# Rearranging the first slots of a fused top-k attention and MLP kernel

## The chip, the cores and the metric

The kernel runs on one core of one Trainium2 chip. The metric is device time in microseconds (us) of one execution, and the median of several runs is compared. Five engines with queues of their own take part: TensorE (PE in the profile), VectorE (DVE), ScalarE (ACT), GpSimd (POOL), and SyncE (SP), which here only issues DMAs. Each works strictly in the order of its queue (weight loads of TensorE can be pulled ahead, row "PEld").

## The reference

For 8 batches of 8 heads, 576 tokens and head size 64: scores, the 32 largest scores of each row kept, softmax over those, times V. The heads are then put side by side (512 features for each of 4608 tokens) and an MLP with 2048 hidden features follows, whose negative half is scaled by a vector alpha.

```
scores = (q @ k.T) / sqrt(64)
kth    = 32nd largest of each row
attn   = softmax(where(scores >= kth, scores, -1e9))
x      = attn @ v                     # heads side by side: 4608 x 512
h      = x @ w_in                     # 4608 x 2048
g      = max(h, 0) + alpha * min(h, 0)
out    = g @ w_out                    # 4608 x 512
```

The kernel writes g as (1 - alpha) * max(h, 0) + alpha * h. The first part uses w_out scaled by (1 - alpha), `w_out_b`. The second is linear in x, so a 512 x 512 matrix `w_lin_b` = w_in (alpha * w_out) is computed once at the start, from `w_la` = alpha * w_out and from a transposed copy of w_in.

## The kernel before, in words

**Units of work.** Two heads form a pair; 4 pairs are a batch, 32 pairs in all. A duo is one 128-row block of both heads of a pair, `("n", pair, j)` with j from 0 to 3, or the 64-row tails of two pairs together, `("m", pair, pair)`. There are 18 duos to a batch and 144 in all; the list `duos` sets their order.

**Slots.** The loop `for n in range(ND + 6)` writes one slot after the other, and each slot touches duos at different stages: scores of duo n+2 on TensorE (`st_qk`, tile `ps_sc`, one buffer); their copy to SBUF on ScalarE for n+1 (`st_exit_1`, `st_exit_0`, tile `s_sb`); the search for the 32nd largest on VectorE (`dve_slot`: twelve MAX8 over 96 columns for duo n, two MAX8 over 576 columns, `p<-y`, for duo n-1); the sign pass `sg` on ScalarE and the product `y` on GpSimd for n-1; `r` on ScalarE and the subtraction `s_sb<-s_sb,r` on GpSimd for n-2; exp (tile `w`) on ScalarE and a DMA transpose of it issued by SyncE (`wT<-w`) for n-3; times V on TensorE (`st_av`, tile `xo`) and the norm on VectorE (`rz`, `x`) for n-5. Every engine has the whole slot in its queue in that order, so a late operand holds all that stands behind it. The instruction `TENSOR_SCALAR p<-small` stands once near the end of VectorE's part of each slot, and its start marks the slot's end in the rows below: there are 144 of them, for slots 0 to 143.

**The MLP beside it.** When both halves of a 256-token chunk are transposed (`st_xT`), `mlp_ready` puts 8 hidden units (`unit`, tile `ph`, 8 matmuls, then one VectorE instruction `gT<-ph`) and 8 output parts (`part`, tile `pz`, 5 matmuls) in lists; `h_pe`, `h_dve` and `o_pe` put about one of each into a slot, two where the list is long. The last two 128-row chunks have 4 units each. What is left when the duos end runs behind the last slot. Where a slot has no unit or part, `keep_warm` puts 4 matmuls in its place (tile `idle`), from slot 4 on.

**Preparing a pair.** `load_one` loads k, q or v (3 DMAs; three staging buffers for k and q, two for v). `prep_pe(p, u)` transposes k (u=0), q (u=1) and both tails (u=2) on TensorE into `tps`, `prep_evac` copies that to `qkT` on ScalarE or VectorE, and `cast_v` casts v on GpSimd, which frees the staging buffer of v.

**The weights.** `out_load(i)` (SyncE) brings 1 MB of w_out to `w_st`, `scale_out(f)` makes one 128x512 block each of `w_out_b` (ScalarE) and `w_la` (VectorE), `w_in_load` (GpSimd's queue) brings w_in, `in_trans` (SyncE) transposes it, `lin` makes `w_lin_b` on TensorE. The dictionary `todo` holds these, filled by `at(slot, kind, f)`; `run(n, kind)` writes them at their place in slot n ("ld" first, "cast" and "prep" late, "scale" last). So SyncE's queue in slot n is: loads of the slot, stores, the transpose of exp(n-3), the transposes of x.

Of the kernel before, what the change touches and what calls it, by code (L numbers as in the profile page):

```python
# [35 lines left out]
def fast_path(tc, q, k, v, moe_w_in, moe_w_out, moe_alpha, out, flag):  # L36
# [17 lines left out]
    for b in range(B):  # L54
        p0 = KPB * b
        full = [("n", p, j) for j in range(4) for p in range(p0, p0 + KPB)]
        tails = [("m", p0, p0 + 1), ("m", p0 + 2, p0 + 3)]
        duos += full + tails if b < B - 1 else tails + full
    ND = len(duos)
# [3 lines left out]
    with ExitStack() as ctx:  # L63
# [3 lines left out]
        io = pool("io", 2)  # L67
        qk_p = pool("qk", 2 * KPB)
        s_p = pool("s", 5)
# [29 lines left out]
        load_one(0, "q", ACT)  # L99
        load_one(1, "k", SP)  # L100
        load_one(1, "q", ACT)

# [334 lines left out]
        def keep_warm():  # L437

            ps = ps_h.tile([128, 512], FP32, name="idle", tag="h")
            for i in range(4):  # L440
                PE.matmul(ps, v1s[0][:, 0, :, :].rearrange("p a b -> p (a b)")[:, 0:128], ws[0][:, 0, 0:512],
                          start=(i == 0), stop=(i == 3))
# [35 lines left out]
        def at(slot, kind, f):  # L478
            todo.setdefault((max(0, slot), kind), []).append(f)

        for b in range(1, B):
            for i in range(KPB):
                p = KPB * b + i
                s0 = NB * (b - 1) + 15 * i // 4
                at(s0 - 6, "ld", lambda p=p: load_one(p, "k"))
                at(s0 - 5, "ld", lambda p=p: load_one(p, "q"))
                at(s0 + 2, "ld", lambda p=p: load_one(p, "v"))
                at(s0 + 5, "cast", lambda p=p: cast_v(p))
                for u in range(3):
                    at(s0 + u, "prep", lambda p=p, u=u: prep_pe(p, u))  # L490
        for p in range(KPB):
            at(p + 1 + p // 2, "cast", lambda p=p: cast_v(p))
            if p > 1:
                at(p, "ld", lambda p=p: load_one(p, "v"))

        def w_in_load(i):
            POOL.dma_start(w_in_b[i], moe_w_in[128 * i:128 * i + 128, :])
# [7 lines left out]
        def scale_out(f):  # L505
            if f % 8 == 0:
                hold["wl", f // 8] = gp.tile([128, 8, 512], BF16, name="w_la", tag="gT")
            src = hold["st", f // 4][:, f % 4, :]
            ACT.activation(w_out_b[f // 4][:, f % 4, :], src, AF.Copy, scale=alpha1m[:, f:f + 1])
            DVE.tensor_scalar(hold["wl", f // 8][:, f % 8, :], src, alpha_sb[:, f:f + 1], None, ALU.mult)  # L510

# [21 lines left out]
        for i in range(4):  # L533
            at((0, 1, 5, 9)[i], "ld", lambda i=i: out_load(i))
            at(3 + 2 * i, "w", lambda i=i: w_in_load(i))
        for f in range(NFT):
            at(1 + f, "scale", lambda f=f: scale_out(f))
        for kk in range(4):
            at((13, 14, 17, 18)[kk], "ld", lambda kk=kk: in_trans(kk))
            for a in range(2):  # L540
                at(16 + 2 * kk + a, "lin", lambda kk=kk, a=a: lin(kk, a))
            at(18 + 2 * kk, "lin_out", lambda kk=kk: lin_out(kk))

# [7 lines left out]

        load_one(2, "k")
        load_one(2, "q")
        load_one(0, "v")
        load_one(3, "k")
        load_one(3, "q")
        load_one(1, "v")

        def prep_all(p, *copies):
            prep_pe(p, 0)  # L560
            prep_pe(p, 1)
            prep_evac(copies[0])
            prep_evac(copies[1])
            prep_pe(p, 2)
            prep_evac(copies[2])


        warm = ps_z.tile([128, 128], FP32, name="warm", tag="z")
        for i in range(12):
            PE.transpose(warm, ident_f, ident_f)  # L570
        prep_all(0, DVE.tensor_copy, ACT.copy, DVE.tensor_copy)
        st_qk(0)
        st_exit_1(0)
        st_exit_0(0)
        prep_all(1, DVE.tensor_copy, ACT.copy, ACT.copy)
        st_qk(1)
        aps = ps_z.tile([128, NFT], FP32, name="aps", tag="z")
        PE.transpose(aps, a16, ident_f[0:NFT, 0:NFT])
        ACT.copy(alpha_sb, aps)
        ACT.activation(alpha1m, aps, AF.Copy, scale=-1.0, bias=1.0)  # L580

        for n in range(ND + 6):
# [5 lines left out]
            if on(n - 5):  # L588
                st_av(n - 5)
            if not h_pe() and not end and n > 3:  # L590
                keep_warm()
# [18 lines left out]
            run(n, "lin_out")  # L610
            if n < 2:
                prep_all(2 + n, ACT.copy, ACT.copy, ACT.copy)
            run(n, "prep", 1)
            if on(n + 2):
                st_qk(n + 2)
            if (n, "lin") in todo:
                run(n, "lin")
            elif not did and not end and n > 3:
                keep_warm()
            elif end or (ready() > 9 and oq[0][1] < NFT):  # L620
                o_pe()
            if on(n - 3):
                st_exp(n - 3)
            while pend:
                prep_evac(ACT.copy)
            run(n, "scale")
# [301 lines left out]
```

## Time and profile before

| what | value |
|---|---|
| runs | 899.44 us median of 3 (898.17, 899.44, 903.78) |
| the profiled execution | 901.29 us, span 899.5 us |
| busy over the span | PE 778.6, DVE 793.8, ACT 791.8, POOL 749.2 us |
| mean granted TensorE clock | 0.952 of full speed |
| busy share of VectorE in 40 slices of 22.5 us | 0.3 and 0.6 in the first two, 0.7 to 0.8 in the next five, 0.9 or more up to the 38th |
| granted clock in those slices | 0.6 to 0.8 in the first seven, 0.9 or more behind |

The profile is of one execution; its times are counted from the start of its span. Busy time is what an engine worked; a wait is put down to the event that ended it. [...]

### The profile page before, as it was taken

How to read it: one execution, taken by the hardware profiler on the slowest of the kernel's cores; microseconds unless marked ns; L12 is line 12 of the kernel's file. 1: busy time of each engine (PE TensorE's matmuls, PEld its weight loads, DVE VectorE, ACT ScalarE, POOL GpSimd, SP SyncE). 2: the span in 40 equal slices, each digit the busy share in tenths (PEclk: the TensorE clock that was granted, in tenths of full speed). 3: DMA queues.
4: the chain of work that ended last, by engine and by line, in shares of the span. 5: the costliest groups of instructions: out<-in, count | busy, mean ns of one | idle time of the engine just before them, and what ended most of it. 6: DMA issues, size and time to landing. Idle time of an engine off the chain costs nothing.

```text
span 899.5 us, 18557 instructions
## 1 busy us (share of the span) xinstructions
PE 778.6 (87%) x5350; PEld 461.3 (51%) x5350; DVE 793.8 (88%) x4063; ACT 791.8 (88%) x1448; POOL 749.2 (83%) x662
## 2 busy tenths in 40 slices
PE   7767777988989889988988899988988999998886
PEld 5423333555555555655455555655555544654553
DVE  3666877899999999999999999999999999999931
ACT  2857787989999999999999999999999999999820
POOL 1766788779999899999999999999998999998910
PEclk6667789999999999999999999999999999999999
DMA  7857675545655556665666465675555444444341
GB/s 159 192 88 140 136 148 114 112 87 91 131 112 109 117 113 121 118 112 103 140 123 116 91 129 104 117 119 112 111 121 108 94 91 93 75 86 77 78 91 39
DMA packets 341006, 99.36 MB, mean 110 GB/s; under 512 B 333712, under 2 KB 333728, under 8 KB 340896
## 3 DMA queue, kind: packets, MB, share of 16 engines
q1 hardware_dynamic: 337888, 95.40, 53.4%
q0 software_dynamic: 608, 2.11, 1.5%
q10 hardware_dynamic: 2400, 0.59, 0.4%
q8 instruction: 44, 0.72, 0.3%
q14 instruction: 66, 0.54, 0.2%
HBM read 36.71 MB, written 9.44 MB: 51 GB/s over the span
## 4 chain that ended last, share of the span: by engine, by line
DVE 33%; ACT 25%; PE 22%; POOL 7%; issue 6%; DMA 5%; SPq 1%; ACTq 0%; POOLq 0%
DVE small L31 9%; DVE p L31 9%; ACT sg L31 7%; PE ps_sc L31 6%; ACT r L31 6%; DVE up L31 5%; ACT w L31 5%; ACT s_sb L31 5%; PE pz L31 5%; POOL y L31 4%; DVE gT L31 4%; PE xo L31 4%; PE ph L31 3%; DMA wT<-w 3%; PE idle L31 2%
## 5 line engine op out<-in xcount | busy, mean ns | idle before, releaser
L31 POOL TENSOR_TENSOR y<-s_sb,sg 128x576 f32<-128x576 f32 x288 | 362.0, 1278 | 89.0 <-ACT sg L31 87.6
L31 POOL TENSOR_TENSOR s_sb<-s_sb,r 128x576 f32<-128x576 f32 x288 | 364.8, 1285 | 19.0 <-ACT r L31 18.2
L31 PE MATMUL ps_sc<-qkT 64*128 64x128 f32 (+7 forms) x1280 | 265.4, 461 | 85.5 <-ACT s_sb L31 82.1
L31 PEld LDWEIGHTS ps_sc<-qkT 64*128 64x128 f32 (+1 forms) x1280 | 148.3, 182 | 227.6 <-ACT s_sb L31 138.2
L31 DVE MAX8 p<-y 128x8 f32<-128x576 f32 x288 | 215.9, 750 | 18.8 <-POOL y L31 18.1
L31 ACT ACTIVATE r<-s_sb,KT 128x576 bf16<-128x576 f32 x288 | 228.4, 794 | 3.8 <-DVE KT L31 2.6
L31 ACT ACTIVATE sg<-s_sb,p 128x576 bf16<-128x576 f32 x288 | 223.1, 786 | 6.2 <-DVE p L31 5.7
L31 DVE MAX8 small<-s_sb 128x8 f32<-128x96 f32 x864 | 217.0, 251 | 0.0
L31 ACT COPY s_sb<-ps_sc 128x576 f32<-128x576 f32 x288 | 184.6, 641 | 34.3 <-PE ps_sc L31 33.3
L31 DVE MAX8 up<-s_sb 128x8 f32<-128x96 f32 x864 | 212.4, 246 | 2.3 <-ACT s_sb L31 2.3
L31 ACT ACTIVATE w<-s_sb 128x1152 bf16<-128x1152 f32 x144 | 168.3, 1169 | 10.3 <-POOL s_sb L31 8.6
L31 PE MATMUL ph<-xT,w_in_b 128*128 128x256 bf16 (+1 forms) x1216 | 150.7, 268 | 0.8 <-DVE gT L31 0.8
L31 PE MATMUL pz<-w_out_b,gT 128*128 128x512 bf16 x576 | 149.6, 383 | 0.0
L31 PE MATMUL xo<-v,wT 128*128 128x65 bf16 (+3 forms) x1600 | 128.7, 200 | 18.6 <-DMA wT<-w 17.0
L31 PEld LDWEIGHTS <-wT 128*128 128x128 bf16 (+3 forms) x1600 | 91.5, 100 | 67.1 <-DMA wT<-w 21.4
L31 PEld LDWEIGHTS <-w_in_b 128*128 128x128 bf16 x1216 | 104.1, 98 | 19.7 <-issue 0.8
L31 DVE TENSOR_SCALAR gT<-ph 128x512 bf16<-128x512 f32 x144 | 97.3, 676 | 18.2 <-PE ph L31 18.1
L31 PEld LDWEIGHTS <-gT 128*128 128x128 bf16 x576 | 56.8, 99 | 57.7 <-issue 6.4
L31 ACT ACTIVATION_READ_ACCUMULATOR sg<-s_sb,p 128x1 f32 x288 | 59.7, 207 | 0.0
L31 PE MATMUL pz<-w_lin_b,xT 128*128 128x512 bf16 x144 | 56.3, 391 | 3.8 <-ACT o_sb L31 3.8
L31 ACT COPY qkT<-tps 128x512 f32<-128x512 f32 (+1 forms) x93 | 44.5, 482 | 6.1 <-PE tps L31 6.0
L31 DVE RECIPROCAL rz<-xo 128x2 f32<-128x2 f32 x144 | 22.7, 157 | 29.6 <-PE xo L31 29.0
(49 smaller groups left out, 592.6 us busy)
## 6 DMA issues: line engine op xcount, KB each, us to landing
k_st<-in_k_dram SPq DMA_DIRECT2D x64, 128.0 KB, 2.8
v_st<-in_v_dram SPq DMA_DIRECT2D x64, 128.0 KB, 2.6
out_dram<-o_sb SPq DMA_DIRECT2D x32, 256.0 KB, 2.5
q_st<-in_q_dram SPq DMA_DIRECT2D x60, 128.0 KB, 2.8
w_st<-in_moe_w_out_dram SPq DMA_DIRECT2D x4, 1024.0 KB, 6.8
wT<-w SPq DMA_TRANSPOSE x144, 3.5
w_in_b<-in_moe_w_in_dram POOLq DMA_DIRECT2D x4, 512.0 KB, 6.6
k_st<-in_k_dram SPq DMA_DIRECT2D x32, 32.0 KB, 2.6
```

The source lines that it names most:

```text
L31: return self.tc.keep_in_program_order(f(*a, **kw))
```

## The change

- **Order of the duos.** Before: row block 0 of the four pairs, then block 1, 2, 3, then the tails. Now: blocks 0 and 1 of a pair in turn, pair by pair, then blocks 2 and 3 the same way, then the tails. In the last batch the tails stood first; now they stand behind blocks 0 and 1, and blocks 2 and 3 follow one by one. A new pair is thus first used every second slot instead of every slot.
- **The opening.** Only pair 0 is prepared ahead of the first scores, and scores of duo 1 (the same pair) come ahead of the transposes of pair 1. `prep_all` for pairs 2 and 3 in slots 0 and 1 is gone; their transposes are spread over slots 0 to 3, two steps a slot. q of pair 1 is loaded by SyncE instead of ScalarE. An Exp on a constant is put first in ScalarE's queue.
- **Loads, casts and transposes.** Slots moved; for all later batches a pair is now prepared every 4 slots. `qk` has 7 buffers instead of 8.
- **The weights.** Loads, `scale_out` (two a slot in slots 3 to 6), `in_trans` and `lin` moved.
- **The alpha product.** The instruction that makes `w_la` sees source and result as 256 x 2 elements, the two 256 columns apart, instead of 512 in a row.
- **keep_warm.** Runs in every slot from 0 on; in slots 0 to 5 it makes 4 transposes of the 128x128 identity instead of 4 matmuls. Ten more warm-up transposes stand in the opening.

```diff
-        full = [("n", p, j) for j in range(4) for p in range(p0, p0 + KPB)]
+        last = b == B - 1
+        half = lambda j, n: [("n", p, j + i) for p in range(p0, p0 + KPB) for i in range(n)]
         tails = [("m", p0, p0 + 1), ("m", p0 + 2, p0 + 3)]
-        duos += full + tails if b < B - 1 else tails + full
+        duos += half(0, 2) + tails + half(2, 1) + half(3, 1) if last else half(0, 2) + half(2, 2) + tails
...
-        qk_p = pool("qk", 2 * KPB)
+        qk_p = pool("qk", 2 * KPB - 1)
...
         load_one(0, "k", SP)
         load_one(0, "q", ACT)
-        load_one(1, "k", SP)
-        load_one(1, "q", ACT)
+        for p in range(1, 3):
+            load_one(p, "k", SP)
+            load_one(p, "q", SP)
+        load_one(0, "v", SP)
...
             for i in range(4):
+                if now[0] < 6:
+                    PE.transpose(ps[:, 128 * i:128 * i + 128], ident_f, ident_f)
+                    continue
...
-                s0 = NB * (b - 1) + 15 * i // 4
-                at(s0 - 6, "ld", lambda p=p: load_one(p, "k"))
-                at(s0 - 5, "ld", lambda p=p: load_one(p, "q"))
+                s0 = NB * (b - 1) + 4 + 4 * i
+                at(s0 - 3, "ld", lambda p=p: load_one(p, "k"))
+                at(s0 - 2, "ld", lambda p=p: load_one(p, "q"))
                 at(s0 + 2, "ld", lambda p=p: load_one(p, "v"))
                 at(s0 + 5, "cast", lambda p=p: cast_v(p))
...
         for p in range(KPB):
-            at(p + 1 + p // 2, "cast", lambda p=p: cast_v(p))
-            if p > 1:
-                at(p, "ld", lambda p=p: load_one(p, "v"))
+            at(2 * p + 2, "cast", lambda p=p: cast_v(p))
+            if p:
+                at(2 * p - 1, "ld", lambda p=p: load_one(p, "v"))
+        for u in range(3):
+            at(u // 2, "prep", lambda u=u: prep_pe(2, u))
+            at(2 + u // 2, "prep", lambda u=u: prep_pe(3, u))
...
-            DVE.tensor_scalar(hold["wl", f // 8][:, f % 8, :], src, alpha_sb[:, f:f + 1], None, ALU.mult)
+
+            DVE.tensor_scalar(hold["wl", f // 8][:, f % 8, :].rearrange("p (a b) -> p b a", a=2),
+                              src.rearrange("p (a b) -> p b a", a=2), alpha_sb[:, f:f + 1], None, ALU.mult)
...
-            at((0, 1, 5, 9)[i], "ld", lambda i=i: out_load(i))
+            at((1, 3, 5, 8)[i], "ld", lambda i=i: out_load(i))
...
-            at(1 + f, "scale", lambda f=f: scale_out(f))
+            at(3 + f // 2 if f < 8 else f - 1, "scale", lambda f=f: scale_out(f))
...
+        ACT.activation(alpha1m, ident_f[:, 0:NFT], AF.Exp)
+        heat(14)
+        for u in range(2):
+            prep_pe(0, u)
+        prep_evac(DVE.tensor_copy)
+        prep_pe(0, 2)
+        prep_evac(ACT.copy)
+        prep_evac(DVE.tensor_copy)
+        heat(6)
+        st_qk(0)
+        load_one(3, "k")
+        load_one(3, "q")
         st_exit_1(0)
         st_exit_0(0)
-        prep_all(1, DVE.tensor_copy, ACT.copy, ACT.copy)
+        heat(2)
         st_qk(1)
+        for u in range(2):
+            prep_pe(1, u)
+        prep_evac(DVE.tensor_copy)
...
-            if not h_pe() and not end and n > 3:
+            if not h_pe() and not end:
                 keep_warm()
...
-            if n < 2:
-                prep_all(2 + n, ACT.copy, ACT.copy, ACT.copy)
-            run(n, "prep", 1)
+            run(n, "prep", 2 if n < 4 else 1)
```

Three places of the queues, before and now. First SyncE's queue from the load of v for pair 3 (slot 3) to the transpose of exp of duo 2 (slot 5) (`v_st`, `k_st`, `q_st` are staging tiles; `w_st` is 1 MB of w_out; `wT<-w` the transposes of exp). Before:

```order
L31 DMA v_st<-in_v_dram 128x4x64 x2
L31 DMA v_st<-in_v_dram 64x2x64
L31 DMA_TRANSPOSE wT<-w_141 128x10x128
L31 DMA_TRANSPOSE wT<-w_142 128x10x128
L31 DMA v_st<-in_v_dram 128x4x64 x2
L31 DMA v_st<-in_v_dram 64x2x64
L31 DMA k_st<-in_k_dram 128x4x64 x2
L31 DMA k_st<-in_k_dram 64x2x64
L31 DMA w_st<-in_moe_w_out_dram 128x4x512
L31 DMA_TRANSPOSE wT<-w_143 128x10x128
```

Now, up to the transpose of exp of duo 3:

```order
L31 DMA w_st<-in_moe_w_out_dram 128x4x512
L31 DMA_TRANSPOSE wT<-w_155 128x10x128
L31 DMA v_st<-in_v_dram 128x4x64 x2
L31 DMA v_st<-in_v_dram 64x2x64
L31 DMA q_st<-in_q_dram 128x4x64 x2
L31 DMA q_st<-in_q_dram 64x2x64
L31 DMA_TRANSPOSE wT<-w_153 128x10x128
```

In the first piece the load ahead of the first transpose is v of pair 3 in slot 3, and the one behind the second is v of pair 5 in slot 5. In the second the v load is that of pair 4 in slot 6, which takes the buffer that the cast of pair 2 frees in the same slot.

TensorE's queue from the first scores on, the first piece of the difference (`warm` and `idle` are transposes of the identity, `tps` transposes of k and q, `ps_sc` scores):

```order
 L31 MATMUL tps<-ident_f,q_st 128x64
+L31 MATMUL warm<-ident_f 128x128 x6
 L31 MATMUL ps_sc<-qkT 128x512
 L31 MATMUL ps_sc<-qkT 128x448
 L31 MATMUL ps_sc<-qkT 128x128
 L31 MATMUL ps_sc<-qkT 128x64
+L31 MATMUL warm<-ident_f 128x128 x2
+L31 MATMUL ps_sc<-qkT 128x512
+L31 MATMUL ps_sc<-qkT 128x448
+L31 MATMUL ps_sc<-qkT 128x128
 L31 MATMUL tps<-ident_f,k_st 128x128 x4
 L31 MATMUL tps<-ident_f,q_st 128x128 x4
```

The scores of duo 1 moved ahead of the transposes of pair 1, and eight identity transposes came in.

VectorE's queue at the end of slot 4 (`pk` is the last small step of a slot, `up<-s_sb` the first MAX8 of the next). Before:

```order
L31 TENSOR_SCALAR w_la<-w_st,alpha_sb 128x512
L31 MAX up<-s_sb 128x8
L31 MAX small<-s_sb 128x8
L31 TENSOR_REDUCE KT<-pk 128x2
L31 MAX up<-s_sb 128x8
```

Now:

```order
L31 TENSOR_SCALAR w_la<-w_st,alpha_sb 128x256x2 x2
L31 MAX up<-s_sb 128x8
L31 MAX small<-s_sb 128x8
L31 TENSOR_REDUCE KT<-pk 128x2
L31 MAX up<-s_sb 128x8
```

Two alpha products stand there in slots 3 to 6, one in slots 7 to 14; before there was one in each of slots 1 to 16. Behind the last scores in TensorE's queue stand 7 units of the 256-token chunks and 25 output parts before, 12 and 26 now; with the 8 units of the last two chunks that is 15 and 20 units.

## Rows read from the trace of the kernel before

**Rows 1.** Windows view: columns stretch, length, busy (instructions) per engine, granted clock, DMA, GB/s.

```profile
17.00:51.00 34.00, 23.40 (x85) 14.28 (x86) 24.36 (x101) 25.46 (x51) 20.14 (x20) 0.65 0.66 154
51.00:103.00 52.00, 35.77 (x165) 17.56 (x164) 34.72 (x173) 35.13 (x64) 33.80 (x35) 0.73 0.75 147
103.00:170.00 67.00, 55.92 (x321) 28.53 (x319) 52.70 (x278) 57.25 (x105) 52.76 (x45) 0.89 0.59 118
```

**Rows 2.** Timeline of VectorE: start, us, then the instruction; ends of slots 0, 20, 118, 119.

```profile
16.94 0.16 DVE L31 TENSOR_SCALAR p<-small 128x2 f32<-128x2 f32 x1
...
169.79 0.14 DVE L31 TENSOR_SCALAR p<-small 128x2 f32<-128x2 f32 x1
...
711.95 0.15 DVE L31 TENSOR_SCALAR p<-small 128x2 f32<-128x2 f32 x1
...
716.68 0.15 DVE L31 TENSOR_SCALAR p<-small 128x2 f32<-128x2 f32 x1
```

**Rows 3.** Waits of VectorE from 17 to 170: us in total, times, longest.

```profile
DVE rz L31 <- PE xo L31: 19.0, 11, 4.2
DVE p L31 <- POOL y L31: 11.0, 15, 2.7
...
DVE w_la L31 <- DMA w_st<-in_moe_w_out_dram: 3.5, 1, 3.5
```

**Rows 4.** Timelines of ScalarE, SyncE and TensorE around the first transpose of exp.

```profile
40.38 1.15 ACT L31 ACTIVATE w<-s_sb 128x1152 bf16<-128x1152 f32 x1
...
51.47 1.57 SPq L31 DMA_DIRECT2D v_st<-in_v_dram  x3
53.14 3.63 SPq L31 DMA_TRANSPOSE wT<-w  x2
...
56.87 1.06 PE L31 MATMUL xo<-v,wT 128*128 128x65 bf16 x10 [4.73 <-DMA wT<-w]
```

**Rows 5.** Timelines of VectorE and GpSimd: alpha products and what GpSimd ran beside one.

```profile
41.85 4.92 DVE L31 TENSOR_SCALAR w_la<-w_st,alpha_sb 128x512 bf16<-128x512 f32 x1
...
60.64 0.48 DVE L31 TENSOR_SCALAR w_la<-w_st,alpha_sb 128x512 bf16<-128x512 f32 x1
...
93.76 2.45 DVE L31 TENSOR_SCALAR w_la<-w_st,alpha_sb 128x512 bf16<-128x512 f32 x1
...
227.99 0.68 DVE L31 TENSOR_SCALAR gT<-ph 128x512 bf16<-128x512 f32 x1
...
41.49 2.52 POOL L31 TENSOR_TENSOR s_sb<-s_sb,r 128x576 f32<-128x576 f32 x2
43.97 2.50 POOL L31 TENSOR_TENSOR y<-s_sb,sg 128x576 f32<-128x576 f32 x2
```

**Rows 6.** Timeline of ScalarE: two exps one slot apart, copy between them, a weight product.

```profile
228.71 1.20 ACT L31 ACTIVATE w<-s_sb 128x1152 bf16<-128x1152 f32 x1
229.77 0.61 ACT L31 COPY qkT<-tps 128x512 f32<-128x512 f32 x1
...
234.17 1.20 ACT L31 ACTIVATE w<-s_sb 128x1152 bf16<-128x1152 f32 x1
...
30.93 0.72 ACT L31 ACTIVATE w_out_b<-w_st,alpha1m 128x512 bf16<-128x512 f32 x1 [0.59 <-DMA w_st<-in_moe_w_out_dram]
```

**Rows 7.** Timeline of TensorE in slots 5 and 6, at either clock.

```profile
61.10 2.29 PE L31 MATMUL ps_sc<-qkT 64*128 64x512 f32 x6 [0.52 <-ACT s_sb L31]
63.32 1.89 PE L31 MATMUL idle<-w,v 128*128 128x512 bf16 x4
65.00 1.09 PE L31 MATMUL xo<-v,wT 128*128 128x65 bf16 x10
...
68.28 1.24 PE L31 MATMUL ps_sc<-qkT 64*128 64x512 f32 x6 [0.73 <-ACT s_sb L31]
```

**Rows 8.** Timeline of TensorE at the end: two units with one part between them.

```profile
847.38 1.05 PE L31 MATMUL ph<-xT,w_in_b 128*128 128x256 bf16 x8
...
849.34 0.93 PE L31 MATMUL ph<-xT,w_in_b 128*128 128x256 bf16 x7
```

More of the change, by code (lines that the diff above doesn't have):

```diff
@@ L533, in fast_path @@
         for i in range(4):
-            at((0, 1, 5, 9)[i], "ld", lambda i=i: out_load(i))
-            at(3 + 2 * i, "w", lambda i=i: w_in_load(i))
+            at((1, 3, 5, 8)[i], "ld", lambda i=i: out_load(i))
+            at((3, 6, 8, 10)[i], "w", lambda i=i: w_in_load(i))
         for f in range(NFT):
-            at(1 + f, "scale", lambda f=f: scale_out(f))
+            at(3 + f // 2 if f < 8 else f - 1, "scale", lambda f=f: scale_out(f))
         for kk in range(4):
-            at((13, 14, 17, 18)[kk], "ld", lambda kk=kk: in_trans(kk))
+            at((11, 12, 15, 16)[kk], "ld", lambda kk=kk: in_trans(kk))
             for a in range(2):
-                at(16 + 2 * kk + a, "lin", lambda kk=kk, a=a: lin(kk, a))
-            at(18 + 2 * kk, "lin_out", lambda kk=kk: lin_out(kk))
+                at(15 + 2 * kk + a, "lin", lambda kk=kk, a=a: lin(kk, a))
+            at(17 + 2 * kk, "lin_out", lambda kk=kk: lin_out(kk))
         def run(n, kind, most=99):
@@ L549, in run, with heat @@
                 todo.setdefault((n + 1, kind), [])[0:0] = l[most:]
-        load_one(2, "k")
-        load_one(2, "q")
-        load_one(0, "v")
+        warm = ps_z.tile([128, 128], FP32, name="warm", tag="z")
+        def heat(m):
+            for _ in range(m):
+                PE.transpose(warm, ident_f, ident_f)
+        ACT.activation(alpha1m, ident_f[:, 0:NFT], AF.Exp)
[8 more added lines that the diff above has]
+        st_qk(0)
         load_one(3, "k")
         load_one(3, "q")
[L557 to L572, printed above, removed]
         st_exit_1(0)
         st_exit_0(0)
-        prep_all(1, DVE.tensor_copy, ACT.copy, ACT.copy)
+        heat(2)
         st_qk(1)
+        for u in range(2):
+            prep_pe(1, u)
+        prep_evac(DVE.tensor_copy)
+        prep_evac(ACT.copy)
+        prep_pe(1, 2)
+        prep_evac(ACT.copy)
         aps = ps_z.tile([128, NFT], FP32, name="aps", tag="z")
         PE.transpose(aps, a16, ident_f[0:NFT, 0:NFT])
-        ACT.copy(alpha_sb, aps)
-        ACT.activation(alpha1m, aps, AF.Copy, scale=-1.0, bias=1.0)
         for n in range(ND + 6):
@@ L617, in fast_path @@
                 run(n, "lin")
-            elif not did and not end and n > 3:
+            elif not did and not end:
                 keep_warm()
@@ L624, in fast_path @@
             while pend:
-                prep_evac(ACT.copy)
+                prep_evac(DVE.tensor_copy if n < 4 and len(pend) == 1 else ACT.copy)
+            if n == 1:
+                ACT.copy(alpha_sb, aps)
+                ACT.activation(alpha1m, aps, AF.Copy, scale=-1.0, bias=1.0)
             run(n, "scale")
```

## The prediction

> **What bounds the kernel now.** I read the 40 slices first: VectorE and ScalarE are full from about 160 us to the end of the slots, and thin before. The windows view puts numbers on the thin stretch [rows 1]: from 17 to 170 us VectorE worked 24.36 + 34.72 + 52.70 = 111.8 of 153 us, ScalarE 117.8 by the same sum, and the granted clock was 0.65, 0.73 and 0.89. Then I took the end of each slot from VectorE's timeline [rows 2]. Slot 0 ends at 16.94 and slot 20 at 169.79, so slots 1 to 20 took 152.9 us, 7.64 each. What a slot needs stands in the same view far behind: slot 119, which has no hidden unit, took 716.68 - 711.95 = 4.73 us without a gap on VectorE. So the opening is the place where time can come from, and a change to the opening can give at most the difference between 152.9 us and what the busiest engine needs there.
>
> That need is ScalarE's. From exp to exp it took 5.46 us with one 0.61 us copy of a transposed q or k in it, 4.85 without [rows 6]. Slots 1 to 20 of the changed kernel hold 20 x 4.85 = 97.0, sixteen weight products of 0.72 [rows 6] = 11.5, and 14 copies that stay on ScalarE, at most 0.61 each, 8.5: 117 us. VectorE needs 111.8 less what it lost in two stretched alpha products (below), about 105. So **the ceiling of the gain is 152.9 - 117 = 36 us**.
>
> Next I read what VectorE waited for [rows 3]: 41.2 us idle (153 - 111.8), of which 19.0 for the product with V (`rz<-xo`), 11.0 for `y`, 3.5 for the first weights. Behind the first of these stands SyncE's queue [rows 4]: exp of duo 0 ended at 41.53, but its transpose was issued at 53.14, right behind a v load that had waited for a buffer. TensorE got it at 56.87. The v load held the transpose for 11.6 us.
>
> **The change part by part,** against the profiled execution of 901.29 us.
>
> *Weights later.* The first `w_st` is loaded in slot 0 and used in slot 1, and VectorE waited 3.5 us [rows 3]. Now two slots lie between load and use: -3.5.
>
> *Loads of v and the transposes behind them.* The v load of slot 3 takes a buffer whose cast is now in slot 2, where before three loads fought for two buffers up to slot 5. One load of this kind is left: v of pair 4 in slot 6 waits for the cast of the same slot, with q of pair 5 and the transpose of exp of duo 3 queued behind it, and TensorE's product in slot 8 waits for that. The 1 MB loads of w_out in slots 5 and 8 also still stand ahead of a transpose. I take half of the 19.0 us [rows 3]: -9.5. Bounds: -19.0 if the queue never blocks again; 0 if the loads left cost what the old ones did.
>
> *Copies ahead of the sign pass.* Six copies for pairs 2 and 3 stood in slots 0 and 1, ahead of `sg`; now they are spread over four slots and VectorE takes some. Of the 11.0 us for `y`, -4; of the idle time that remains (41.2 - 19.0 - 11.0 - 3.5 = 7.7, much of it where TensorE prepares two pairs in a row), -4. Bounds together 0 and -18.7.
>
> *The alpha product.* Fourteen of the sixteen took about what the one at 60.64 took, 0.48; two took 4.92 and 2.45 [rows 5]. The long one ran from 41.85 to 46.77, while GpSimd worked without a gap from 41.49 to 46.47: VectorE stood until GpSimd was done. 0.48 us for 512 elements is also short of the 0.68 that 512 elements from PSUM take [rows 5], so it runs in a faster form that seems to need something GpSimd holds. The two cost 4.44 + 1.97 = 6.4 us. If the new view ends that, -6.4; if the product then takes 0.68, it costs 16 x 0.20 = +3.2. Bounds for one product: 0.48, as now, and 4.92, the longest seen. I take 0.68, the nearest row for 512 elements one by one.
>
> [...]
>
> *The first microseconds.* VectorE now copies a part of pair 1 ahead of its slot 0, and the scores of duo 1 (1.24 us at full clock, 2.29 at half [rows 7]) stand ahead of those transposes; against it, ScalarE is ready earlier because it issues three DMAs fewer. I take +1.5, bounds -1.2 and +4.
>
> *More keep_warm.* Eight identity transposes a slot in slots 0 to 3. Eight matmuls of 512 columns took at most 2 x 1.89 [rows 7], which is the upper bound; TensorE had 34.0 - 23.4 = 10.6 us free from 17 to 51 [rows 1], 2.6 a slot. I cost them at nothing while that holds; without it at 1.2 a slot, 5 in all.
>
> *Between slot 21 and the last batch.* The work of a batch is the same and the spacing of loads 4 slots instead of 3.75: 0, bounds -4 and +3.
>
> *The end.* The last batch's tails now become ready behind blocks 0 and 1, so 5 more units and 1 more part run after the last scores. A unit and a part took 849.34 - 847.38 = 1.96 there, a further unit at most 1.05 [rows 8]: 1.96 + 4 x 1.05 = +6.2 where TensorE sets the end. The slots lose 5 VectorE instructions of 0.68 [rows 5], up to -3.4. I take +3.5, bounds +2.8 and +6.2.
>
> Sum: -3.5 - 9.5 - 4 - 4 - 6.4 + 3.2 + 1.5 + 0 + 3.5 = **-19.2**, so 882.1 for an execution like the profiled one. That one lay 1.85 above the median of the runs, 899.44, so the median should be about **880**.
>
> **The rivals.**
>
> 1. *The alpha product still waits for GpSimd* (the change doesn't do what it says). For it: nothing in the trace shows that it was the order of the elements that let it run in 0.48 us; and with shorter slots GpSimd, 106.7 of 153 us busy by the sum of its column [rows 1], would be nearer 85%, and two products now stand together in slots 3 to 6. Against it: the time of a strided stream is not in the trace. Five long products instead of two, at the mean loss of (4.44 + 1.97) / 2 = 3.2 us, cost 16.0, against a gain of 6.4 less 3.2 in my sum: 882.1 + 16.0 - 3.2 = 895 in the profile if nothing hides it, and about 888 where ScalarE hides half; median 887. Chance 0.15. [...]
>
> 2. *The waits move.* ScalarE or TensorE comes late in place of the queue, and the three middle terms (17.5) give half: +8.8, profile 891, median 889. For it: a chain through TensorE, ScalarE and GpSimd runs through each early slot, and a wait removed shows the next. Against it: the ceiling of 36 us is far above what I take. Chance 0.17.
>
> 3. *TensorE at half clock becomes the bound: slower.* The place is slots 6 to 18, where two `idle` groups a slot remain. [...] It decides where the mean granted clock of that stretch falls below about 0.7. For it: the clock was 0.73 from 51 to 103, and the new fillers of slots 0 to 5 are short transposes. Against it: it rose to 0.89 behind [rows 1], as the gaps on TensorE became shorter, and the change makes gaps shorter. Chance 0.08.
>
> **How the numbers follow.** My forecast has 0.60. The low end is the ceiling: 36 us less, the same work at the end, a median near 864. The high end takes in rivals 1 and 2 with their bounds, 897; it leaves out rival 3 and a little at both ends. A difference of under 1%, 9 us, I count as no change: that is, faster means below 890.4. The forecast lies there nearly wholly (0.57 of 0.60), rival 1 with 0.10 of 0.15, rival 2 with 0.08 of 0.17. Faster 0.75, within 1% 0.17, slower 0.08.
>
> **What would show it.** In the changed profile slot 20 should end near 146 to 150 instead of 169.79; the first transpose of exp should be issued within 2 us of its exp; no alpha product should last over 1 us; `rz<-xo` should hold VectorE for about 10 us in the opening, with its longest wait near slot 8; the stretch behind the last slot should be 4 to 6 us longer than now. The prediction is wrong if slot 20 ends after 160, if the alpha products are stretched as before, or if the slots between 21 and 125 change their pace, of which I count on nothing.

## The result, and the profile after

The changed kernel took **876.1 us** (median of 4 runs, 874.74 to 877.41) against 899.63 (4 runs, 898.17 to 903.78): a ratio of **0.9729, interval 0.9699 to 0.976**. The profiled execution took 874.74 us with a span of 873.0 (901.29 and 899.5 before), at a mean granted clock of 0.973 (0.952). The forecast was 880. The time came out near it, but two of its terms were wrong by over ten microseconds each, in opposite directions, and the experiments were spent on that.

The timeline of VectorE in the changed kernel gives the ends of slots 0, 3, 20, 125 and 143, which answer to [rows 2] (start, duration, instruction):

```profile
16.84 0.16 DVE L31 TENSOR_SCALAR p<-small 128x2 f32<-128x2 f32 x1
...
31.93 0.14 DVE L31 TENSOR_SCALAR p<-small 128x2 f32<-128x2 f32 x1
...
151.72 0.14 DVE L31 TENSOR_SCALAR p<-small 128x2 f32<-128x2 f32 x1
...
725.45 0.14 DVE L31 TENSOR_SCALAR p<-small 128x2 f32<-128x2 f32 x1
...
822.30 0.15 DVE L31 TENSOR_SCALAR p<-small 128x2 f32<-128x2 f32 x1
```

In the kernel before, slots 0 and 20 end at 16.94 and 169.79 [rows 2], and slots 3, 125 and 143 here:

```profile
41.63 0.14 DVE L31 TENSOR_SCALAR p<-small 128x2 f32<-128x2 f32 x1
...
750.90 0.14 DVE L31 TENSOR_SCALAR p<-small 128x2 f32<-128x2 f32 x1
...
848.99 0.14 DVE L31 TENSOR_SCALAR p<-small 128x2 f32<-128x2 f32 x1
```

Set beside each other, the two sets of five divide the 26.5 us of the span:

| stretch | before, us | after, us | difference |
|---|---|---|---|
| to the end of slot 0 | 16.94 | 16.84 | -0.1 |
| slots 1 to 3 | 24.69 | 15.09 | -9.6 |
| slots 4 to 20 | 128.16 | 119.79 | -8.4 |
| slots 21 to 125 | 581.11 | 573.73 | -7.4 |
| slots 126 to 143 | 98.09 | 96.85 | -1.2 |
| behind the last slot | 50.51 | 50.70 | +0.2 |

The windows view of the changed kernel, for slots 1 to 20, answers to [rows 1] (stretch, length, busy time of PE, PEld, DVE, ACT and POOL with instructions, granted clock, DMA share, GB/s):

```profile
17.00:51.00 34.00, 22.85 (x120) 15.03 (x117) 33.69 (x136) 26.99 (x52) 25.49 (x23) 0.80 0.66 163
51.00:103.00 52.00, 40.95 (x210) 20.87 (x209) 49.59 (x199) 41.19 (x75) 45.99 (x38) 0.77 0.82 158
103.00:152.00 49.00, 42.41 (x255) 22.29 (x255) 43.96 (x222) 45.77 (x84) 41.81 (x36) 0.93 0.58 115
```

VectorE, the third figure, is now full in the first two stretches: 33.69 of 34 and 49.59 of 52. By the sum it worked 127.2 of 135 us, where it had worked 111.8 of 153. So its idle time fell from 41.2 to 7.8 us, **33.4 less**, while its busy time rose by **15.4**. The gain of these slots, 18.0 us, is the difference of the two. What is left of the idle time stands in VectorE's waits from 17 to 152 (us in total, times, longest), against [rows 3]:

```profile
DVE p L31 <- POOL y L31: 2.9, 7, 1.2
DVE rz L31 <- PE xo L31: 2.6, 4, 1.1
DVE small L31 <- ACT sg L31: 1.6, 3, 0.9
```

The wait for the product with V went from 19.0 to 2.6, that for `y` from 11.0 to 2.9, and that for the first weights is gone. The busy time is the alpha products'. The groups view of VectorE in the same stretches shows their sum and the mean of one, first before, then in the changed kernel:

```profile
L31 DVE TENSOR_SCALAR w_la<-w_st,alpha_sb 128x512 bf16<-128x512 f32 x16 | 14.8, 924 | 3.5 <-DMA w_st<-in_moe_w_out_dram 3.5
```

```profile
L31 DVE TENSOR_SCALAR w_la<-w_st,alpha_sb 128x512 bf16<-128x512 f32 x16 | 34.5, 2267 | 0.0
```

Their rows grew by 19.7 us. That is more than the 15.4 by which the busy time rose, because 3.9 us more of them overlap the rows of neighbouring instructions.

The timelines of VectorE and GpSimd show two kinds of product, and answer to [rows 5]:

```profile
32.34 7.03 DVE L31 TENSOR_SCALAR w_la<-w_st,alpha_sb 128x512 bf16<-128x512 f32 x2
...
58.04 4.13 DVE L31 TENSOR_SCALAR w_la<-w_st,alpha_sb 128x512 bf16<-128x512 f32 x2
...
73.56 1.54 DVE L31 TENSOR_SCALAR w_la<-w_st,alpha_sb 128x512 bf16<-128x512 f32 x1
...
88.19 3.51 DVE L31 TENSOR_SCALAR w_la<-w_st,alpha_sb 128x512 bf16<-128x512 f32 x1
...
34.27 2.50 POOL L31 TENSOR_TENSOR y<-s_sb,sg 128x576 f32<-128x576 f32 x2
40.44 2.55 POOL L31 TENSOR_TENSOR s_sb<-s_sb,r 128x576 f32<-128x576 f32 x2 [3.67 <-ACT r L31]
42.92 0.85 POOL L31 CAST v<-v_st 128x512 bf16<-128x512 f32 x2
...
58.98 3.34 POOL L31 CAST v<-v_st 128x512 bf16<-128x512 f32 x2
```

No product took under 1.5 us; the shortest took 1.54, three times the 0.48 of before. The pair at 32.34 took 7.03 beside a product `y` that kept its usual 2.50: VectorE stood. GpSimd was then idle for 3.67 us, because the `r` that it needed waited for VectorE. Beside the pair at 58.04 it was the other way round: two casts of v took 3.34 us, against 0.85 at 42.92, and GpSimd stood. So the two engines still hold each other up, and the new element order made each product longer.

The queue of SyncE, on the other hand, did what the prediction said. ScalarE's exp of duo 0 and SyncE's transpose of it, which answer to [rows 4]:

```profile
30.70 1.15 ACT L31 ACTIVATE w<-s_sb 128x1152 bf16<-128x1152 f32 x1
```

```profile
31.87 3.91 SPq L31 DMA_TRANSPOSE wT<-w  x1
```

Exp ended at 31.85 and the transpose was issued at 31.87, where before 11.6 us lay between.

Last, the windows view behind the last slot, of before and of the changed kernel:

```profile
849.00:899.50 50.50, 38.58 (x314) 23.32 (x312) 13.92 (x35) 11.08 (x17) 8.00 (x7) 0.96 0.27 64
```

```profile
822.30:873.00 50.70, 43.36 (x356) 27.33 (x354) 17.22 (x40) 11.19 (x17) 7.78 (x7) 0.97 0.30 68
```

TensorE did 4.8 us more work there, its first figure, in a stretch that grew by 0.2: it had 11.9 us of gaps before and has 7.3 now.

### The profile page after: what moved, and what is told of

Same layout as the page of the kernel before. It is cut to its first block, busy times and chain, and to the rows that moved or that the text cites. A ratio compares the mean times of both kernels' runs of the same rounds, so it can differ in the third digit from the quotient of the medians.

```text
span 873.0 us, 18673 instructions
## 1 busy us (share of the span) xinstructions
PE 770.9 (88%) x5400; PEld 461.1 (53%) x5400; DVE 808.7 (93%) x4067; ACT 789.1 (90%) x1445; POOL 756.6 (87%) x662
## 4 chain that ended last, share of the span: by engine, by line
DVE 43%; ACT 21%; PE 20%; POOL 8%; issue 5%; DMA 2%; SPq 1%; ACTq 0%; POOLq 0%
DVE small L31 12%; DVE p L31 12%; DVE up L31 7%; ACT sg L31 6%; PE ps_sc L31 6%; DVE gT L31 5%; PE pz L31 5%; POOL y L31 5%; ACT r L31 5%; ACT w L31 4%; ACT s_sb L31 4%; PE ph L31 4%; POOL s_sb L31 2%; PE xo L31 2%; PE plin L31 1%
## 5 line engine op out<-in xcount | busy, mean ns | idle before, releaser
L31 PE MATMUL ps_sc<-qkT 64*128 64x128 f32 (+7 forms) x1280 | 260.1, 453 | 88.9 <-ACT s_sb L31 87.4
L31 PEld LDWEIGHTS ps_sc<-qkT 64*128 64x128 f32 (+1 forms) x1280 | 145.0, 179 | 230.1 <-ACT s_sb L31 148.8
L31 PE MATMUL pz<-w_out_b,gT 128*128 128x512 bf16 x576 | 147.8, 379 | 0.0
L31 ACT COPY o_sb<-pz 128x512 f32<-128x512 f32 x36 | 21.6, 599 | 30.9 <-PE pz L31 30.9
```

Of the source, the lines that this page charges most:

```text
L31: return self.tc.keep_in_program_order(f(*a, **kw))
```

## The experiments

Each kernel bears on one question; every ratio is against runs of the kernel before on the same chip. Where a slot or an instruction is named, it is that of the profiled execution.

### What the alpha product's new view is worth

**The changed kernel with the old, flat product:**

```diff
-            DVE.tensor_scalar(hold["wl", f // 8][:, f % 8, :].rearrange("p (a b) -> p b a", a=2),
-                              src.rearrange("p (a b) -> p b a", a=2), alpha_sb[:, f:f + 1], None, ALU.mult)
+            DVE.tensor_scalar(hold["wl", f // 8][:, f % 8, :], src, alpha_sb[:, f:f + 1], None, ALU.mult)
```

> The changed kernel with the alpha product on 512 elements in a row again. Theory A (the 256 x 2 view makes each product about 1.4 us instead of 0.5 and does not end the waiting for GpSimd; VectorE is the full engine of the new opening): the twelve groups of products shrink from 34.5 us to 15 to 20, slot 20 ends 4 to 10 us earlier than 151.72, median 866 to 872. Theory B (the view is needed, flat products would stand behind GpSimd more often): groups over 40 us in all, median above 880. Theory C (ScalarE hides the products): 874 to 878.

Measured: 870.17 us (867.42 to 870.99), ratio 0.9646 (0.96 to 0.9692). Slot 20 ends at 147.03 instead of 151.72, with 3.8 of the 4.7 us in slots 4 to 8. VectorE's group shows what changed:

```profile
L31 DVE TENSOR_SCALAR w_la<-w_st,alpha_sb 128x512 bf16<-128x512 f32 x16 | 19.8, 1255 | 0.0
```

The sixteen products fell from 34.5 to 19.8 us; the first pair still took 5.11, another 2.92. So the view made the kernel slower by 5.9 us (876.1 - 870.17), or by 4.1 against a second set of runs of the changed kernel (874.25, below; its slot 20 ended at 149.79). The flat product was stretched as before.

**The kernel before with the new view,** nothing else (the same two lines the other way round):

> The kernel before with nothing but the 256 x 2 view. Theory A: each of the 16 products takes 1.3 to 1.6 us when GpSimd is idle and still stretches beside it; 15 us more on VectorE, of which its 41 us of idle time in the opening hide half or more: 3 to 8 us slower than before, 903 to 908. Theory B: the two stretched products of 4.92 and 2.45 us go, nothing over 1 us is left: 893 to 897.

Measured: 902.9 us (900.41 to 908.23), ratio 1.0024 (1.0 to 1.0048). The group:

```profile
L31 DVE TENSOR_SCALAR w_la<-w_st,alpha_sb 128x512 bf16<-128x512 f32 x16 | 32.4, 2025 | 3.2 <-DMA w_st<-in_moe_w_out_dram 3.2
```

The products that had taken 4.92 and 2.45 took 5.94 and 3.51 here, a third 2.33, and each of the others 1.51 to 1.66. The sum rose from 14.8 to 32.4 us, but the time by 2 only, if at all, a little under what theory A expected: VectorE was idle for 41 us of these slots, which left room for this work. The view lengthens the products' rows by 14.7 us in the changed kernel (34.5 - 19.8) and by 17.6 in this one; only in the changed one is VectorE near full.

**The changed kernel with a flat product that also writes out its sum** (into a tile that nothing reads):

```diff
+        al_acc = const.tile([128, NFT], FP32, name="al_acc")
...
-            DVE.tensor_scalar(hold["wl", f // 8][:, f % 8, :].rearrange("p (a b) -> p b a", a=2),
-                              src.rearrange("p (a b) -> p b a", a=2), alpha_sb[:, f:f + 1], None, ALU.mult)
+            DVE.tensor_scalar(hold["wl", f // 8][:, f % 8, :], src, alpha_sb[:, f:f + 1], None, ALU.mult, op1=ALU.add,
+                              accum_out=al_acc[:, f:f + 1])
```

> The changed kernel with the alpha product on 512 elements in a row and a sum output added that nothing reads. [...]

Measured: **866.67 us** (864.2 to 868.39), ratio **0.9616** (0.9568 to 0.9664), the shortest of all kernels here; slot 20 ends at 142.30. The groups of VectorE, where the product now has another name and a second row for the sum:

```profile
L31 DVE TENSOR_SCALAR_CACHE_REDUCE w_la<-w_st,alpha_sb 128x512 bf16<-128x512 f32 x16 | 11.5, 738 | 0.0
L31 DVE DVE_READ_ACCUMULATOR w_la<-w_st,alpha_sb 128x1 f32 x16 | 1.3, 83 | 0.0
```

All sixteen took 0.73 to 0.74 us, and none was stretched, although GpSimd worked for 104.0 of the 125.3 us from 17 us to the end of slot 20. That is what the new view was to do: a product a little slower than 0.48 us that isn't stretched beside GpSimd. The first pair took 5.11 us with the flat product and 7.03 with the viewed one. Why this form isn't stretched no run shows.

### What the load of v in SyncE's queue was worth

**The kernel before, v of batch 1 loaded and cast four slots later:**

```diff
-                at(s0 + 2, "ld", lambda p=p: load_one(p, "v"))
-                at(s0 + 5, "cast", lambda p=p: cast_v(p))
+                late_v = 4 if b == 1 else 0
+                at(s0 + 2 + late_v, "ld", lambda p=p: load_one(p, "v"))
+                at(s0 + 5 + late_v, "cast", lambda p=p: cast_v(p))
```

> The kernel before with one edit: v of pairs 4 to 7 is loaded and cast four slots later, so that no v load stands blocked in SyncE's queue ahead of a transpose of exp. Theory H (that queue made the late products with V): first transpose of exp issued before 45 us instead of 53.14, VectorE's wait for the product with V falls from 19.0 to under 9 us, slot 20 ends 5 to 10 us earlier than 169.79, median 890 to 895. Rival (the 1 MB loads and TensorE's clock hold it anyway): slot 20 within 3 us of 169.79, median 897 to 900.

Measured: 890.2 us (888.4 to 891.28), ratio 0.9886 (0.9854 to 0.9919), where the kernel before had 901.32 beside it: two lines give 11.1 us. SyncE's queue in this kernel, with exp of duo 0 ending at 42.28:

```profile
39.02 1.57 SPq L31 DMA_DIRECT2D v_st<-in_v_dram  x3
42.31 1.51 SPq L31 DMA_TRANSPOSE wT<-w  x1
```

Its transpose is issued 0.03 us after exp, against 11.6 [rows 4]. VectorE's wait for the product with V from 17 to 158 us, first in the kernel before, then here:

```profile
DVE rz L31 <- PE xo L31: 18.0, 10, 4.2
```

```profile
DVE rz L31 <- PE xo L31: 5.2, 6, 1.6
```

So 12.8 us of it hung on these loads, and slot 20 ended 12.3 us sooner. The prediction's -9.5 for this term was a fair size; what it missed lay beside it.

### What moved the slots between 21 and 143

The changed kernel was 7.4 us shorter from slot 20 to 125, where the prediction counted on nothing. **Old order of row blocks in batches 1 to 6,** the rest as changed:

```diff
+        full = half(0, 1) + half(1, 1) + half(2, 1) + half(3, 1)
-        duos += half(0, 2) + tails + half(2, 1) + half(3, 1) if last else half(0, 2) + half(2, 2) + tails
+        duos += half(0, 2) + tails + half(2, 1) + half(3, 1) if last else (half(0, 2) + half(2, 2) if b == 0 else full) + tails
```

> The changed kernel with the old order of duos (row block by row block, then tails) in batches 1 to 6; the opening and the last batch as changed. Theory F (the new order is what made slots 28 to 125 4.7 us shorter, 532.8 instead of 537.5): they take 536 to 538, median 3 to 5 us above that of the changed kernel. Theory G (the even spacing of the preparing did it): they take 532 to 534, median 874 to 878.

Measured: 874.1 us (873.14 to 881.42), ratio 0.9724 (0.9669 to 0.978). Slots 21 to 125 took 573.76 us, 573.73 with the new order. Behind batch 0, the order by itself moves nothing.

**Old spacing of the transposes** from batch 3 on (with the 8 `qk` buffers of before; k and q are still loaded 3 and 2 slots ahead):

```diff
-        qk_p = pool("qk", 2 * KPB - 1)
+        qk_p = pool("qk", 2 * KPB)
...
-                s0 = NB * (b - 1) + 4 + 4 * i
+                s0 = NB * (b - 1) + (4 + 4 * i if b < 3 else 15 * i // 4)
```

> The changed kernel with pairs of batches 3 to 7 prepared at the old spacing of 3.75 slots, so three pairs nearly without a slot between them and earlier in the batch (8 qkT buffers, since a pair is then kept longer). Theory G: slots 41 to 125 take 466 to 468 us, as before the change (467.7), instead of 462.6; median 3 to 6 us above the changed kernel. Theory F: 462 to 464, no change.

Measured: 886.05 us (883.38 to 888.02), ratio 0.9829 (0.979 to 0.9868). Slots 42 to 125 took 466.40 us, 457.23 in the changed kernel and 461.85 before. (The theories counted one slot more: by that count it is 471.85 here, above the 466 to 468 of theory G, with 462.56 and 467.73 in the other two.) TensorE's waits over these slots, first in the kernel before (290 to 751 us), then here (268 to 735); the changed kernel has none for `wT`:

```profile
PE xo L31 <- DMA wT<-w: 5.7, 4, 1.8
```

```profile
PE xo L31 <- DMA wT<-w: 8.1, 5, 2.3
```

The longest of the five, in the timelines of SyncE, ScalarE (an exp that ends at 670.70) and TensorE:

```profile
668.89 1.76 SPq L31 DMA_DIRECT2D v_st<-in_v_dram  x3
670.69 2.63 SPq L31 DMA_DIRECT2D q_st<-in_q_dram  x3
673.42 0.54 SPq L31 DMA_DIRECT2D out_dram<-o_sb  x1
674.07 3.15 SPq L31 DMA_TRANSPOSE wT<-w  x2
...
669.53 1.17 ACT L31 ACTIVATE w<-s_sb 128x1152 bf16<-128x1152 f32 x1
...
678.04 0.79 PE L31 MATMUL xo<-v,wT 128*128 128x65 bf16 x10 [2.29 <-DMA wT<-w]
```

Issuing loads of v and q and a store kept SyncE from 668.89 to 673.96, and the transpose of an exp that was ready at 670.70 was issued at 674.07. The same slot of the kernel before (exp ends at 684.62):

```profile
682.54 1.75 SPq L31 DMA_DIRECT2D v_st<-in_v_dram  x3
684.33 1.79 SPq L31 DMA_DIRECT2D k_st<-in_k_dram  x3
...
686.86 1.40 SPq L31 DMA_TRANSPOSE wT<-w  x1
...
683.45 1.17 ACT L31 ACTIVATE w<-s_sb 128x1152 bf16<-128x1152 f32 x1
...
691.40 0.79 PE L31 MATMUL xo<-v,wT 128*128 128x65 bf16 x10 [1.74 <-DMA wT<-w]
```

This row of TensorE multiplies by what the transpose at 686.86 brought. By the same rows of the other batches the transposes of the sixth slot of a batch (slots 59, 77, 95 and 113) were issued 2.3 to 2.6 us behind their exp before and 2.6 to 3.4 here; in the changed kernel none of slots 42 to 125 was more than 1.5 us late. So the middle's gain is again SyncE's queue: with the new places no transpose there held TensorE up. Whether the spacing does it or the place in the batch isn't separated, as the edit also moves each pair 4 or 5 slots earlier. The experiment overshoots (it is slower than before), and its loads stand 3 and 2 slots ahead of the transposes instead of 6 and 5, so it gives the mechanism and not the size of the term.

**Old order in the last batch,** with the old spacing for its pairs and 8 buffers:

```diff
-        duos += half(0, 2) + tails + half(2, 1) + half(3, 1) if last else half(0, 2) + half(2, 2) + tails
+        duos += tails + half(0, 1) + half(1, 1) + half(2, 1) + half(3, 1) if last else half(0, 2) + half(2, 2) + tails
...
-        qk_p = pool("qk", 2 * KPB - 1)
+        qk_p = pool("qk", 2 * KPB)
...
-                s0 = NB * (b - 1) + 4 + 4 * i
+                s0 = NB * (b - 1) + (4 + 4 * i if b < B - 1 else 15 * i // 4)
```

> The changed kernel with the old order of the last batch (tails first, then row block by row block; its pairs prepared at the old spacing, 8 qkT buffers). Theory I (TensorE's idle time behind the last slot takes the 5 more units in): the stretch behind the last slot stays at 49 to 52 us, the last batch's slots are about 1 us longer, median within 2 us of the changed kernel. Rival J (units behind the last slot cost their full time): the stretch is 4 to 6 us shorter, median 2 to 5 us below.

Measured: 882.76 us (879.12 to 884.97), ratio 0.9794 (0.9751 to 0.9836), which none of the theories had. It falls apart by place: slot 20 ended 3.6 us later (2.1 of it in slot 0, below), slots 109 to 118, where the old spacing stands, took 3.4 us more, and slots 126 to 143 took 98.07 against 96.85. The stretch behind the last slot was 50.46 against 50.70. So the new order of the last batch is worth 1.2 us in the slots and costs 0.2 behind them. At the old spacing it is worth 1.9 (98.07 here, 96.14 in the kernel above), so the new spacing takes 0.7 of it back.

**Eight `qk` buffers alone,** to see whether the buffers and not the spacing cost the time of the last two kernels:

```diff
-        qk_p = pool("qk", 2 * KPB - 1)
+        qk_p = pool("qk", 2 * KPB)
```

> The changed kernel with 8 buffers for transposed q and k instead of 7, nothing else. The runs with the old 3.75-slot spacing of the loads also had 8 buffers, so their loss (+10 us with the old spacing from batch 3 on, +6.7 in the last batch alone) could be the buffers' and not the spacing's. Theory S (spacing): 876 us, 874 to 878, and slots 41 to 125 take 457 us as in the changed kernel. Theory Q (buffers): 880 us or more, with slots 41 to 125 over 461. If the first scores run at half clock here by chance, slot 0 ends about 2 us later and the time is 2 us above, in both theories.

Measured: 875.47 us (874.51 to 878.42), ratio 0.9729 (0.9713 to 0.9745): the buffers cost nothing by the median. The profiled execution was the longest of the four and had slots 42 to 125 at 460.82, 3.6 above the changed kernel, between the two expectations; 2.9 of that are three waits of VectorE for the product with V. The kernel with the old last batch settles it: it has 8 buffers too, with the new spacing for all but the last batch's pairs, and took 364.38 us for slots 42 to 108, against 364.46 in the changed kernel. So the 3.6 us are a matter of the single execution and not of the buffers, and as much of the 9.2 us of the old spacing could be chance.

### The first microseconds

**The changed kernel without the identity transposes** of slots 0 to 5 and the ten more of the opening (the 12 of before stay):

```diff
-        heat(14)
+        heat(12)
...
-        heat(6)
...
-        heat(2)
...
-                if now[0] < 6:
-                    PE.transpose(ps[:, 128 * i:128 * i + 128], ident_f, ident_f)
-                    continue
...
-            if not h_pe() and not end:
+            if not h_pe() and not end and n > 3:
...
-            elif not did and not end:
+            elif not did and not end and n > 3:
```

> The changed kernel without the identity transposes of slots 0 to 5 and of the opening (keep_warm from slot 4 on with matmuls, 12 warm-up transposes, as before). Theory D (they hold the clock up: 1.00 up to 28 us against 0.50 from 9 to 32 before, and that makes slots 1 to 3 short): clock near 0.5 from 10 to 30 us, six score matmuls 2.29 us instead of 1.24, slot 3 ends 4 to 8 us later than 31.93, median 879 to 884. Rival E (the order of the transposes alone made slots 1 to 3 short): slot 3 ends within 2 us of 31.93, median 874 to 878.

Measured: 876.63 us (875.66 to 877.22), ratio 0.9719 (0.9677 to 0.9762): no difference that can be told. Slot 0 ended at 19.36 instead of 16.84, and slots 1 to 3 took 15.07 against 15.09. So the short slots 1 to 3 are not the fillers' doing. Nor are they the v loads', whose move alone left these slots at 25.69 us, 24.69 before. The order, the spread transposes and the later weights remain (VectorE's wait of 3.5 us [rows 3] lay in these slots), and no run separates them. The 2.5 us of slot 0 I first put down to the fillers, until the two kernels with 8 buffers and old spacing, which have all fillers and the same opening, ended slot 0 at 18.72 and 18.96. **The changed kernel once more,** unedited:

> The changed kernel once more, to see whether the clock of the first 12 us is a matter of chance. Slot 0 ended at 16.84 us in the changed kernel, 16.95 with the old order of row blocks, but at 19.36 without the identity transposes, and at 18.96 and 18.72 in two kernels that have all of them and the same opening. Theory C (chance): median again 876 (874 to 878), slot 0 ends anywhere from 16.4 to 19.4, and runs differ by up to 3 us. Theory F (the fillers hold the clock and the two late kernels differ in something else): slot 0 ends at 16.8 to 17.0 again. One profile that gives 16.8 can't tell them apart; one that gives 19 speaks for C.

Measured: 874.25 us (873.82 to 875.54), ratio 0.9724 (0.9708 to 0.974); slot 0 ended at 16.54. TensorE's first transposes of k and first scores, in this run, in the changed kernel's first run, and in the one with the old last batch:

```profile
5.26 0.63 PE L31 MATMUL tps<-ident_f,k_st 128*128 128x128 f32 x4 [0.64 <-DMA k_st<-in_k_dram]
...
7.75 1.24 PE L31 MATMUL ps_sc<-qkT 64*128 64x512 f32 x6
```

```profile
5.09 1.09 PE L31 MATMUL tps<-ident_f,k_st 128*128 128x128 f32 x4 [0.47 <-DMA k_st<-in_k_dram]
...
8.04 1.24 PE L31 MATMUL ps_sc<-qkT 64*128 64x512 f32 x6
```

```profile
5.08 1.09 PE L31 MATMUL tps<-ident_f,k_st 128*128 128x128 f32 x4 [0.47 <-DMA k_st<-in_k_dram]
...
8.83 2.24 PE L31 MATMUL ps_sc<-qkT 64*128 64x512 f32 x6
```

In the first of these both run at the short durations, in the second the transposes take longer, and in the third both do; for the scores they are close to the two rows in [rows 7], where the granted clock read 1.00 (68.28 to 69.50) and 0.50 (61.10 to 63.30). Of the nine profiled executions with all fillers, seven had the first scores at 1.24 us and two at over 2; of the four without them (before, two edits of it, and this one) none. That leans towards the fillers, but it is a matter of chance in each execution, is worth 2 us at most, and stays open.

### Can the best version be made shorter?

**The kernel with the sum-writing product, v loads of batch 1 one slot later:**

```diff
-                at(s0 + 2, "ld", lambda p=p: load_one(p, "v"))
+                at(s0 + (3 if b == 1 else 2), "ld", lambda p=p: load_one(p, "v"))
```

> The kernel with the alpha product in the form that also writes a sum (866.67 us) with the v loads of batch 1 one slot later, so that none stands in SyncE's queue ahead of the cast that frees its buffer. Theory 1 (a load that waits in SyncE's queue still holds transposes of exp): the rz waits of the opening fall from 5.2 us in all to about 3, 864 to 865 us. Theory 2 (ScalarE and VectorE are the bound of the opening now, 122.6 and 117.8 us of work to slot 20's end at 142.3): no change that can be told, 866 to 867, and the idle time of VectorE goes to the product y or the sign pass instead. I expect theory 2 with 0.65.

Measured: 868.11 us (866.26 to 869.43), ratio 0.9656 (0.964 to 0.9672). That is above the 866 to 867 of theory 2, but not apart from the 866.67 of the kernel without this edit, whose interval it overlaps. The waits speak for theory 2: VectorE's wait for the product with V fell from 5.2 to 4.9 us only, where theory 1 asked for about 3, and that for `y` rose from 7.7 to 9.1. The windows view of the kernel without this edit, from 17 us to the end of slot 20 (columns as in [rows 1]):

```profile
17.00:142.30 125.30, 101.87 (x572) 57.78 (x577) 109.90 (x567) 113.06 (x209) 104.01 (x96) 0.88 0.76 155
```

ScalarE worked 113.1 and VectorE 109.9 of the 125.3 us, so little is left that one late queue could give back.

## Why the prediction came out right, and where it was wrong

| term | predicted | measured in the profiled executions |
|---|---|---|
| weights, v loads, copies: waits of VectorE in slots 1 to 20 | -21.0 | -33.4 |
| alpha product | -3.2 | busy time of VectorE in these slots +15.4 |
| first microseconds | +1.5 | -0.1 |
| slots 21 to 125 | 0 | -7.4 |
| last batch and the end | +3.5 | -1.0 |
| sum | -19.2 | -26.5 |

- **The place was right.** Slots 1 to 20 gave 18.0 of the 26.5 us. The mechanism named, transposes of exp that no longer stand behind a load of v, is shown: moving these loads alone in the kernel before gave 11.1 us, beside the -9.5 of the term, all of it behind slot 3. The 9.6 us of slots 1 to 3 come from other parts of the change, which were not tried one by one.
- **The waits were undersized.** The prediction took half of the 19.0 us for the product with V, because loads were left ahead of a transpose, and 4 of the 11.0 for `y`. Nearly all went: 16.4 and 8.1. The one load that was to block still did (v of pair 4 issued at 62.34, the transpose behind it at 65.88, its exp ended at 60.64), but VectorE was by then late itself, through the alpha products, and waited 1.1 us at most. So a part of these waits was only covered by longer products: in the kernel with the sum-writing product VectorE was idle for 15.4 us of the same slots (125.3 - 109.9), against 7.8 here. By that kernel the waits fell by 25.8 us, 4.8 more than predicted.
- **The alpha product failed, and with it a stated condition.** The step was "if the new view ends that", and it did not. Rival 1 had the mechanism, at a chance of 0.15. That it is the fast form of 0.48 us that needs something GpSimd holds, no run shows: the viewed product, never under 1.5 us, was stretched too, to 5.94. The price of a strided product, taken as 0.68 by the nearest row, was 1.54 at the shortest. Against a product that isn't stretched the view costs the whole kernel 9.4 us (876.1 - 866.67), against the flat one 5.9; against the second set of runs it is 7.6 and 4.1. Rival 1 priced five long products at 16.0; the product rows grew by 34.5 - 14.8 = 19.7 us.
- **The time was near by luck.** The two errors cover each other: 12.4 us too little for the waits, 18.6 too little for the products. The prediction priced each by itself, and nothing in it made them cancel. How full VectorE was decided what a product costs: with its idle time nearly gone, 14.7 us less of the products gave 4.1 to 5.9 us and 23.0 less (34.5 - 11.5) gave 7.6 to 9.4, about a third, where in the kernel before 17.6 us more of them moved the time by 2. The middle (-7.4) and the end (-4.5 against its term) then took it below the forecast.
- **The middle** was said to keep pace and didn't. The spacing had been costed at 0 since the work is the same; the place of a load in SyncE's queue is not. 2.9 of the 4.6 us of slots 42 to 125 are VectorE's waits for the product with V, 3.3 before and 0.4 now. That was the second of the three signs of being wrong that it gave itself, beside the stretched products. The 2.8 us of slots 21 to 41 lie in batches whose spacing no experiment undid; their cause is open.
- **The end** was costed as if TensorE were full behind the last slot. It had 11.9 us of gaps there, and the extra units went into them.
- **The other signs.** The first transpose came 0.02 us behind its exp, as said. Slot 20 ended at 151.72, just behind the 146 to 150; `rz<-xo` held VectorE for 2.6 us instead of about 10, longest not near slot 8 but at 113 us, in slot 14; the stretch behind the last slot grew by 0.2 instead of 4 to 6.
- **Rival 3** didn't come: the granted clock of 0.77 from 51 to 103 us stayed above its 0.7, which was the author's estimate.

## What to carry to other kernels

When a rearrangement takes waits away, price every instruction it lengthens on an engine that may be nearly full behind it: here about a third of the added length came out as time, in the kernel before, with the engine idle for a quarter of the stretch, a ninth. In these kernels the place of each load in SyncE's queue was a matter of the whole kernel (11.1 us for two lines): look for the load that stands ahead of a transpose whose input is nearly ready. Where a VectorE product is stretched beside GpSimd, try another form of the instruction, and read from one run whether that ends it: here the form that writes out its sum took 0.738 us in the mean, none of sixteen stretched, while with another order of the elements a pair took 7.03.

## What the runs showed of the hardware

- A product of 128x512 from float32 to bfloat16 in SBUF took 0.48 us flat, 0.74 (and 0.08 for reading the sum) in the form that writes out its sum, and 1.51 to 1.66 viewed as 256 x 2 with both sides hopping by 256 columns, where nothing stretched it. The flat and the viewed one were stretched beside GpSimd, to 4.92 and 5.94 us for the same product of the kernel before; the sum-writing one was not in any of its 16 products, at 0.73 to 0.74 us. Which of the two sides that hop costs the time no run separates.
- It went both ways: two casts on GpSimd took 3.34 us beside a viewed pair, 0.85 without.
- The same first matmuls took longer or shorter from one execution to the next: 1.24 or 2.24 us for six matmuls of scores, 0.63 or 1.09 for four transposes of k. The granted clock from 5 to 6 us read 1.00 in the changed kernel, where those transposes took 1.09, and 1.00 in the kernel before, where they took 0.63. So that column doesn't show there what the rows show, and the cause is open.
